# The first sixteen weight pieces on a denser timetable, and v loaded one slot later, in a fused sigmoid attention and bilinear FFN kernel

## The chip, the cores and the metric

The kernel runs on one core of a Trainium2 chip. The metric is device microseconds of one execution. The kernel before was run three times: 1097.2, 1098.67 and 1100.7 us, median 1098.67 us.

## The reference

Float32 throughout. Eight batches of 12 heads, 448 positions, 64 values per head; then an FFN without activation on the 3584 tokens.

```python
scores = scale * np.matmul(q, k.transpose(0, 1, 3, 2)) - np.log(S)
attn = 1.0 / (1.0 + np.exp(-scores))
attn_out = np.matmul(attn, v).astype(np.float32)
x = np.ascontiguousarray(attn_out.transpose(0, 2, 1, 3)).reshape(B * S, H * D)
...
a = x @ w1
b = x @ w2
h = a * b @ w3
return (h @ w_out).astype(np.float32)
```

The weights w1, w2 (768 x 1024), w3 and w_out reach the kernel as the 32-bit words of 64-bit floating point numbers, and the kernel turns them into float32 itself.

## The kernel before, in words

**Attention.** Two heads make a pair, six pairs a batch, 48 pairs in all. A pair's 448 keys are cut into chunks of 128, 128, 128 and 64, taken in the order first, short, second, third. One chunk of one pair is a *slot*; slot number = 4 x pair + place of the chunk. In a slot PE does the score matmuls of its chunk into one of two PSUM tiles `sp` (`scores`, L196 or L199), ACT takes their sigmoid (`attention`, L180), and one slot later PE multiplies it with v (`attend`, L248 or L255, called attend matmuls here). After a pair's last chunk `combine` writes its part of x as a high half `xh` (ACT, L66) and a low half `xl` (DVE, L67).

The first nine pairs (`PLAIN = 9`, slots 0 to 35) do this with plain float32 operands. From pair 9 on (slot 36) every operand is split into a high and a low part: `split_pair` makes qs, kh, kl (DVE L158, L159, L66, POOL L67), `split_v` makes vs, and the sigmoid is taken twice so that DVE can form `al` (L217); the short chunk goes another way (`short_scores` L225, `short_attention` with L187 and L239).

**The up projection.** From slot 26 on, 12 matmuls of `up` (L320) fill each slot: they multiply the x of the batch before with w1 and w2, column block by column block, three slots each. ACT copies one product (`a_sb`, L328), DVE multiplies (`g`, L331), and g goes to DRAM.

**The weights.** w1 and w2 come in 16 pieces: piece 2f is column block f of w1, piece 2f+1 that of w2. `decode_weights` is a generator with two steps a piece. In its first step it issues the load of words to come, lets ACT take the magnitude of this piece and of the next if their words are on the way (`f<-raw`, L79), and issues six DVE instructions (the decode: L86, L91, L94, L98, L99, L102). In its second step it splits the result, with the high half written by ACT (`w<-f`, L66) and the low half by DVE (`w<-f`, L67). The magnitudes lie in two buffers `f`, so the magnitude of a piece waits until the split of the piece two before is over. Pieces 0 to `EARLY - 1` are loaded two pieces ahead into three buffers (768 KB each); the others, and the 16 half-size pieces of w3T that follow, share one buffer, and the load of each stands in the program behind the decode of the piece before.

**What sets the order.** SP (which issues every load and store), PE, ACT and POOL take their instructions in the order in which the program is written, ACT and POOL only until slot 32; the order of DVE, and from slot 32 on that of ACT and POOL, is made by a scheduler when the kernel is built. The list `starts` (L346) gives the slots in which the 16 pieces take their first step, `steps` (L349) adds the second steps (two slots later in the first batch, one later in the second), and `take(weights, steps.count(slot))` (L418) runs them, in each slot behind the sigmoid of that slot. `EARLY` (L351) is worked out from `starts`. `prepare` (L380 on) issues the loads of the pairs to come: q and k two pairs ahead, v one pair ahead into one of two buffers. At slot 32 the three buffers of the early words are given up, and the split operands of pair 9 take their place.

After the attention come the last batch's up projection, w3 times w_out, and the product of g with it.

Of the kernel before, what the change touches and what calls it, by code (L numbers as in the profile page):

```python
# [25 lines left out]
def sigmoid_attention_bilinear_ffn(  # L26
# [29 lines left out]
    PLAIN = 9  # L56
# [66 lines left out]
    def load_pair(b, hp):  # L123
        heads = slice(2 * hp, 2 * hp + 2)
        if b * NPAIR + hp < PLAIN:

            qk = pa.tile([P, 2, S], F32, name="qp", tag="qk", bufs=3)
            for i, src in enumerate((qT, kT)):
                nc.sync.dma_start(out=qk[:, i], in_=src[b, heads].rearrange("h d s -> (h d) s"))
            return qk[:, 0], qk[:, 1]  # L130
        qq = pa.tile([P, 2, S], F32, name="qq", tag="qk", bufs=3)
        kk = pa.tile([P, 2, S], F32, name="kk", tag="qk", bufs=3)
        for dst, src in ((qq, qT), (kk, kT)):
            for r in range(2):
                nc.sync.dma_start(
                    out=dst[r * D:(r + 1) * D], in_=src[b, heads].rearrange("h d s -> d h s")
                )
        return qq, kk

    def load_v(b, hp):  # L140
        vv = pa.tile([P, NC, 2 * D], F32, name="vv")
        cols = slice(hp * 2 * D, (hp + 1) * 2 * D)
        full = (NC - 1) * P
        nc.sync.dma_start(
            out=vv[:, :NC - 1], in_=v[b, :full, cols].rearrange("(c p) e -> p c e", p=P)
        )
        for r in range(1 if b * NPAIR + hp < PLAIN else 2):
            nc.sync.dma_start(out=vv[r * D:(r + 1) * D, NC - 1], in_=v[b, full:, cols])
        return vv

    def split_pair(plain, qq, kk):

        if plain:
            return qq, kk, None, None
        qs = pf[0].tile([P, 2, S], F32R, name="qs")
        kh = pf[0].tile([P, 2, S], F32R, name="kh")
        kl = pf[0].tile([P, 2, S], F32R, name="kl")
        nc.vector.tensor_copy(out=qs, in_=qq)  # L158
        nc.vector.tensor_tensor(out=qs[D:], in0=qq[D:], in1=qs[D:], op=ALU.subtract)  # L159
        split(kh, kl, kk, nc.vector.tensor_copy, nc.gpsimd)  # L160

        ks = pf[0].tile([P, 2, P], F32R, name="ks")
        for j in range(2):
            for i, k in ((j, kh), (1 - j, kl)):
                nc.gpsimd.tensor_copy(out=ks[:, j, i * D:(i + 1) * D], in_=k[:, j, S - D:])
        return qs, kh, kl, ks

    def split_v(plain, vv):
        if plain:
            return vv  # L170

        vs = pf[0].tile([P, NC, 2, 2, D], F32R, name="vs")
        for j in range(2):
            split(vs[:, :, j, j, :], vs[:, :, j, 1 - j, :], vv[:, :, j * D:(j + 1) * D],
                  nc.vector.tensor_copy, nc.gpsimd)
        return vs
# [166 lines left out]
    pairs = [(b, hp) for b in range(B) for hp in range(NPAIR)]  # L343

    first = NPAIR * NC
    starts = [1 + i * first // 7 for i in range(7)] + [first + 1 + 3 * i // 2 for i in range(8)] + [first + 14]  # L346
    assert len(starts) == 2 * NF
    later = [(2 * NPAIR + 2 * i) * NC + 1 for i in range(2 * NF)]
    steps = starts + [s + 2 - s // first for s in starts] + later  # L349
# [29 lines left out]
    def prepare(p, i):  # L379

        n = p + 1
        change = n in (PLAIN, PLAIN + 1)
        if i == (2 if change else 1) and n < len(pairs):
            splits[n] = split_pair(n < PLAIN, *qks.pop(n))
        if i == 0 and change:
            qks[n] = load_pair(*pairs[n])
        if i == (0 if n < PLAIN else 1) and n < len(pairs):
            vvs[n] = load_v(*pairs[n])
        if i == NC - 1 and n < len(pairs):
            vs[n] = split_v(n < PLAIN, vvs.pop(n))  # L390
        n = p + 2
        if i == (0 if n < PLAIN else 2) and n not in (PLAIN, PLAIN + 1) and n < len(pairs):
            qks[n] = load_pair(*pairs[n])
# [6 lines left out]
    for p, (b, hp) in enumerate(pairs):  # L400
        if p == PLAIN - 1:
            order.close()
            order.enter_context(tc.manual_schedule(engines={ET.PE, ET.SP}))
        plain = p < PLAIN
        if p == PLAIN - 1:
            phase_p.close()
            pf.append(phase_a.enter_context(tc.tile_pool(name="pf", bufs=2, side="right")))
        qs, kh, kl, ks = splits.pop(p)
        for i, c in enumerate(chunks):
            prepare(p, i)  # L410
            if not plain and i == 1:
                short = short_scores(ks, qs)
            else:
                sp = scores(qs, kh, kl, c)
                if not plain and i == 2:
                    waiting.append((slot + 1, p, NC - 1, short_attention(short)))
                waiting.append((slot + 1, p, c, attention(plain, sp)))
            take(weights, steps.count(slot))  # L418
            if b > 0 and (hp, i) == (0, 2):
                take(filler, 10 ** 6)  # L420
                filler = up(b - 1, xs[b - 1], itertools.repeat("up"))
            take(filler, ups)
            attend_due(slot)
            slot += 1
# [124 lines left out]
```

## Time and profile before

| | us |
|---|---|
| median of three runs (lowest, highest) | 1098.67 (1097.2, 1100.7) |
| the profiled execution, its own time | 1100.9 |
| its span in the profile | 1099.0 |
| PE busy | 1072.5 |
| DVE busy | 717.4 |
| ACT busy | 564.0 |
| POOL busy | 196.8 |
| granted clock of PE, mean | 0.992 of full |

The span is the profiled execution from its first to its last instruction; 1.9 us lie around it. PE is TensorE's matmuls, PEld its weight loads, DVE VectorE, ACT ScalarE, POOL GpSimd, and SPq the queue through which SyncE issues DMAs. A row of the timeline has the start in us from the span's beginning, the duration, the engine, the line of the code, the operation, what it writes and reads, and in brackets how long the engine had been idle before it and what ended that. A row of the waits has who waited for whom, then the sum in us, the count and the longest. A row of a group has the number of instructions behind the x, the busy time, the mean in ns, and the idle time before. "DMA to landing" is the time from a load's issue to the arrival of its last byte, as lowest, median and highest of the loads asked for. The slots can be found on PE by their score matmuls: slot 9 starts at 24.56, slot 10 at 30.64, slot 26 at 61.95, slot 36 at 106.98, slot 38 at 122.79, slot 40 at 134.15, slot 44 at 158.33 and slot 48 at 173.89 us.

### The profile page before, as it was taken

Reading aid. Unit: us, or ns where it says so; the run is one execution under the profiler, and the core shown is the slowest. Engines: PE = TensorE matmul, PEld = TensorE weight load, DVE = VectorE, ACT = ScalarE, POOL = GpSimd, SP = SyncE. Lnnn points to the kernel's source line nnn. Section 1 sums busy time; section 2 is a strip of 40 time slices with the busy share of each in tenths; the row PEclk is TensorE's granted clock in tenths of the full one; section 3 lists DMA queues with packets and bytes.
Section 4 is the critical chain, followed back from the end, with each engine's and each line's share of the span. In section 5 each row is a group of like instructions: output and inputs, shape, how many; then the busy total and the mean of one; then the engine's idle time right before and its main releaser. Section 6 shows DMA issues by size and latency. Waiting matters only on the chain.

```text
span 1099.0 us, 14114 instructions
## 1 busy us (share of the span) xinstructions
PE 1072.5 (98%) x5076; PEld 913.8 (83%) x5076; DVE 717.4 (65%) x1073; ACT 564.0 (51%) x789; POOL 196.8 (18%) x277
## 2 busy tenths in 40 slices
PE   7999689999999999999999999999999999999998
PEld 1255579999999999899999999999999988888887
DVE  5878787878888887888888877758872122122221
ACT  5753557776677777667776677753342011011100
POOL 0002142333223332332323233300000000000000
PEclk9999899999999999999999999999999999999999
DMA  7562633544444444452543524206462031333211
GB/s 240 165 195 89 151 116 95 132 116 123 114 121 132 114 125 123 108 153 73 151 121 99 161 83 109 73 20 209 140 222 79 10 125 59 123 125 125 86 49 48
DMA packets 100693, 129.15 MB, mean 118 GB/s; under 512 B 8016, under 2 KB 82960, under 8 KB 100624
## 3 DMA queue, kind: packets, MB, share of 16 engines
q1 hardware_dynamic: 100624, 128.25, 39.8%
q8 instruction: 40, 0.66, 0.3%
q14 instruction: 29, 0.24, 0.1%
HBM read 98.34 MB, written 29.88 MB: 117 GB/s over the span
## 4 chain that ended last, share of the span: by engine, by line
PE 85%; DVE 6%; DMA 4%; ACT 2%; issue 2%; SPq 1%; POOL 0%; DVEq 0%; ACTq 0%
PE up L320 38%; PE up L510 21%; PE av L255 10%; PE sp L199 8%; PE up L494 6%; DMA raw<-w 3%; PE sp L225 1%; DVE f L94 1%; ACT f L79 1%; DVE raw L99 1%; DVE f L102 1%; PE av L248 1%; DVE w L67 1%; PE sp L196 1%; DVE raw L86 0%
## 5 line engine op out<-in xcount | busy, mean ns | idle before, releaser
L320 PE MATMUL up<-xh,w 128*128 128x448 f32 x1536 | 469.9, 369 | 1.8 <-DVE g L331 1.8
L320 PEld LDWEIGHTS up<-xh,w 128*128 128x128 f32 x1536 | 290.2, 189 | 34.8 <-issue 5.3
L320 PE MATMUL up<-xl,w 128*128 128x448 f32 x768 | 282.7, 368 | 0.0
L510 PE MATMUL up<-w 128*128 128x512 f32 x1008 | 228.7, 389 | 0.0
L510 PEld LDWEIGHTS up<-w 128*128 128x128 f32 x1008 | 189.2, 188 | 39.3
L180 ACT ACTIVATE ah<-sp,bias 128x896 fp32r<-128x896 f32 x117 | 117.5, 1004 | 114.5 <-PE sp L199 113.7
L67 POOL TENSOR_TENSOR kl<-kk,kh 128x896 fp32r<-128x896 f32 x39 | 88.5, 2268 | 417.9 <-DVE kh L66 401.9
L217 DVE TENSOR_TENSOR al<-sp,ah 128x896 fp32r<-128x896 f32 x117 | 127.3, 1088 | 48.1 <-ACT sp L180 46.7
L320 PEld LDWEIGHTS up<-xl,w 128*128 128x128 f32 x768 | 145.1, 189 | 13.0
L520 DVE COPY o_sb<-up 128x512 f32<-128x512 f32 x42 | 29.0, 690 | 161.1 <-PE up L510 161.1
L66 ACT CAST w<-graw 128x1024 fp32r<-128x1024 f32 x28 | 29.3, 1055 | 174.6 <-PE up L510 170.5
L180 ACT ACTIVATE sp<-sp,bias 128x896 f32<-128x896 f32 x117 | 113.6, 971 | 0.1
L255 PE MATMUL av<-ah,vs 128*128 128x448 f32 x312 | 102.7, 369 | 3.1 <-DVE ah L239 1.3
L199 PE MATMUL sp<-qs,kh 128*128 128x448 f32 x234 | 86.7, 370 | 4.1 <-DVE kh L66 2.4
L67 POOL TENSOR_TENSOR vs<-vv,vs 128x256 fp32r<-128x256 f32 x78 | 70.9, 919 | 99.5 <-DVE vs L66 82.4
L199 PE MATMUL sp<-qs,kl 128*128 128x448 f32 x234 | 86.8, 371 | 1.9 <-POOL kl L67 1.9
L255 PE MATMUL av<-al,vs 128*128 128x448 f32 x234 | 86.0, 368 | 2.1 <-DVE al L217 2.1
L239 DVE TENSOR_TENSOR ah<-st,ah 64x448 fp32r<-64x448 f32 x78 | 57.6, 739 | 21.0 <-ACT st L180 19.2
L255 PEld LDWEIGHTS av<-ah,vs 128*128 128x128 f32 x312 | 58.7, 188 | 10.3 <-issue 3.5
L79 ACT ACTIVATE f<-raw 128x768 f32<-128x768 f32 (+2 forms) x48 | 34.0, 708 | 61.7 <-DMA raw<-w_out 20.7
L186 ACT COPY t<-av 64x448 f32<-64x448 f32 x78 | 41.2, 528 | 33.6 <-PE av L255 32.5
L180 ACT ACTIVATE ah<-st,bias 64x448 fp32r<-64x448 f32 x78 | 52.2, 669 | 4.0 <-DVE st L187 2.1
(54 smaller groups left out, 1249.0 us busy)
## 6 DMA issues: line engine op xcount, KB each, us to landing
qq<-qT SPq DMA_DIRECT2D x78, 224.0 KB, 3.9
kk<-kT SPq DMA_DIRECT2D x78, 224.0 KB, 4.4
g_dram<-g SPq DMA_DIRECT2D x64, 224.0 KB, 2.0
graw<-g_dram SPq DMA_DIRECT2D x14, 1024.0 KB, 5.4
raw<-w SPq DMA_DIRECT2D x16, 768.0 KB, 6.5
out<-o_sb SPq DMA_DIRECT2D x42, 256.0 KB, 2.0
vv<-vL SPq DMA_DIRECT2D x48, 192.0 KB, 2.7
raw<-w3T SPq DMA_DIRECT2D x16, 512.0 KB, 4.3
```

Source lines behind the costliest of these rows:

```text
L66: hi_engine(out=dst_hi, in_=src)
L67: lo_engine.tensor_tensor(out=dst_lo, in0=src, in1=dst_hi, op=ALU.subtract)
L79: nc.scalar.activation(f, raw[..., 1].bitcast(F32), AF.Abs, scale=HW_SCALE)
L180: nc.scalar.activation(dst, src, AF.Sigmoid, bias=bias[:n], scale=scale)
L186: nc.scalar.copy(out=dst[rows], in_=src[j][others])
L199: nc.tensor.matmul(sp[:, j], k[:, j, at:at + n], qs[:, j], start=m == 0, stop=m == 1)
L217: nc.vector.tensor_tensor(out=al, in0=sp, in1=ah, op=ALU.subtract)
L239: nc.vector.tensor_tensor(out=a[others, j], in0=t[rows], in1=a[rows, j], op=ALU.subtract)
L255: nc.tensor.matmul(accs[j][:, :S], v[:, c, j].rearrange("p u d -> p (u d)"), a[:, j], start=first and m == 0, stop=last and m == len(ops) - 1,
L320: nc.tensor.matmul(acc[:, :S], w[:, fc, kc], x, start=(kc == 0 and m == 0), stop=(kc == NK - 1 and m == 2),)
L494: nc.tensor.matmul(acc[:, :NM], a[:, jc], w[:, jc, ms], start=(jc == 0 and m == 0), stop=(jc == NF - 1 and m == 2),)
L510: nc.tensor.matmul(acc[:, :TB], w[:, fc, ms], g[:, at, fc % NH], start=(fc == 0 and m == 0), stop=(fc == NF - 1 and m == 2),)
```

## The change

```diff
     first = NPAIR * NC
-    starts = [1 + i * first // 7 for i in range(7)] + [first + 1 + 3 * i // 2 for i in range(8)] + [first + 14]
+    starts = [1 + 3 * i for i in range(8)] + [first + 1 + 4 * i // 3 for i in range(8)]
     assert len(starts) == 2 * NF
...
         if i == 0 and change:
             qks[n] = load_pair(*pairs[n])
-        if i == (0 if n < PLAIN else 1) and n < len(pairs):
+        if i == 1 and n < len(pairs):
             vvs[n] = load_v(*pairs[n])
```

The first steps of the 16 pieces move from slots 1, 4, 7, 11, 14, 18, 21, 25, 26, 28, 29, 31, 32, 34, 35, 38 to slots 1, 4, 7, 10, 13, 16, 19, 22, 25, 26, 27, 29, 30, 31, 33, 34. The second steps move from 3, 6, 9, 13, 16, 20, 23, 26, 27, 29, 30, 32, 33, 35, 36, 39 to 3, 6, 9, 12, 15, 18, 21, 24, 26, 27, 28, 30, 31, 32, 34, 35. `EARLY` becomes 14 instead of 12. The w3T pieces keep their slots. The loads of v for the first nine pairs are issued in the second slot of the pair before instead of its first; those of the later pairs were there already.

On SP, in slots 4 to 7: `qp` is q and k of pair 3, `vv` is v of pair 2, `raw` on w2 is piece 3's words, and the row ahead of them is piece 2's. Before:

```order
L74 DMA raw_122<-w1 128x6x256
L144 DMA vv_153<-vL 128x3x128
L148 DMA vv_153<-vL 64x128
L129 DMA qp_156<-qT 128x448
L129 DMA qp_156<-kT 128x448
L74 DMA raw_164<-w2 128x6x256
```

After:

```order
L74 DMA raw_122<-w1 128x6x256
L129 DMA qp_153<-qT 128x448
L129 DMA qp_153<-kT 128x448
L74 DMA raw_161<-w2 128x6x256
L144 DMA vv_177<-vL 128x3x128
L148 DMA vv_177<-vL 64x128
```

The loads of v, which need the buffer of pair 0's v, moved from ahead of q, k and piece 3's words to behind them.

On DVE, around slot 36, whose `al` is the L217 row. `f_730` and `f_769` are pieces 13 and 14 before; a `w` row is the low half of a split. Before:

```order
L102 TENSOR_TENSOR f_730<-f_730,raw_663 128x768
L331 TENSOR_TENSOR g_752<-up_703,a_sb_701 128x448
L67 TENSOR_TENSOR w_90<-f_730,w_89 128x768
L86 TENSOR_SCALAR raw_738<-raw_738 128x768
L91 TENSOR_SCALAR f_769<-f_769 128x768
L94 SCALAR_TENSOR_TENSOR f_769<-f_769,raw_738 128x768
L98 TENSOR_SCALAR raw_738<-f_769 128x768
L217 TENSOR_TENSOR al_808<-sp_800,ah_805 128x896
L99 SCALAR_TENSOR_TENSOR raw_738<-raw_738 128x768
L67 TENSOR_TENSOR xl_830<-av_710,xh_829 128x448
L102 TENSOR_TENSOR f_769<-f_769,raw_738 128x768
```

After, where `f_707` is piece 14, `f_754` is piece 15 and `raw_762` the first piece of w3T:

```order
L102 TENSOR_TENSOR f_707<-f_707,raw_640 128x768
L66 CAST vs_781<-vv_698 128x4x64
L67 TENSOR_TENSOR w_88<-f_707,w_87 128x768
L331 TENSOR_TENSOR g_776<-up_725,a_sb_723 128x448
L86 TENSOR_SCALAR raw_715<-raw_715 128x768
L91 TENSOR_SCALAR f_754<-f_754 128x768
L94 SCALAR_TENSOR_TENSOR f_754<-f_754,raw_715 128x768
L98 TENSOR_SCALAR raw_715<-f_754 128x768
L99 SCALAR_TENSOR_TENSOR raw_715<-raw_715 128x768
L102 TENSOR_TENSOR f_754<-f_754,raw_715 128x768
L67 TENSOR_TENSOR w_90<-f_754,w_89 128x768
L217 TENSOR_TENSOR al_822<-sp_814,ah_819 128x896
```

The end of piece 14 and all of piece 15, which stood behind slot 36's al, now stand ahead of it; behind it the first w3T piece follows at once.

On DVE in the first batch, the rows at the turn from one piece to the next, where `f_248` is piece 4, `f_291` piece 5 and `raw_289` the words of piece 6; after:

```order
L102 TENSOR_TENSOR f_291<-f_291,raw_246 128x768
L67 TENSOR_TENSOR w_88<-f_248,w_87 128x768
L86 TENSOR_SCALAR raw_289<-raw_289 128x768
L67 TENSOR_TENSOR xl_339<-av_299,xh_338 128x448
L91 TENSOR_SCALAR f_328<-f_328 128x768
```

and before, at the same turn:

```order
L102 TENSOR_TENSOR f_299<-f_299,raw_253 128x768
L67 TENSOR_TENSOR w_88<-f_255,w_87 128x768
L67 TENSOR_TENSOR xl_332<-av_289,xh_331 128x448
L86 TENSOR_SCALAR raw_297<-raw_297 128x768
L91 TENSOR_SCALAR f_350<-f_350 128x768
```

The xl of a pair moved at this turn from ahead of the next piece's decode to inside it; the split of piece 4 stays behind the decode of piece 5 in both.

## The prediction

> **What bounds the kernel now.** I read the page's busy shares first, then the table of windows, cut at the score matmuls of slots 26, 36, 44 and 48.
>
> ```profile
> span 1099.0 us, 14114 instructions
> PE 1072.5 (98%) x5076; PEld 913.8 (83%) x5076; DVE 717.4 (65%) x1073; ACT 564.0 (51%) x789; POOL 196.8 (18%) x277
> ```
>
> ```profile
> 0.00:61.95 61.95, 52.15 (x204) 12.97 (x204) 43.96 (x62) 40.84 (x49) 0.20 (x4) 0.97 0.65 202
> 61.95:106.98 45.03, 45.03 (x202) 26.50 (x201) 34.49 (x50) 20.82 (x27) 5.02 (x6) 1.00 0.50 142
> 106.98:158.33 51.35, 39.13 (x155) 31.71 (x154) 41.55 (x57) 26.28 (x36) 13.62 (x16) 0.87 0.45 119
> 158.33:173.89 15.56, 15.56 (x78) 14.26 (x76) 12.36 (x20) 10.74 (x15) 6.03 (x8) 1.00 0.41 115
> 173.89:700.00 526.11, 525.40 (x2568) 481.58 (x2567) 428.88 (x642) 375.54 (x534) 167.26 (x238) 1.00 0.44 118
> ```
>
> The columns are the stretch, its length, then busy time of PE, PEld, DVE, ACT and POOL, granted clock, DMA share, GB/s. From slot 44 (158.33) on, PE has no gap, so whatever moves slot 44 moves the end by as much. Slots 26 to 36 are full too (45.03 of 45.03, 4.50 a slot). The loss is elsewhere: 9.8 us of PE idle before slot 26, and slots 36 to 44 took 51.35 where eight later slots take 2 x 15.56 = 31.1: 20.2 us. The change touches only these stages. Next the timeline of the first loss:
>
> ```profile
> 17.31 0.38 SPq L144 DMA_DIRECT2D vv<-vL  x1
> 19.43 1.08 SPq L74 DMA_DIRECT2D raw<-w  x2
> 23.61 0.95 DVE L67 TENSOR_TENSOR w<-f,w 128x768 fp32r<-128x768 f32 x1
> 24.56 0.97 PE L196 MATMUL sp<-qp 64*64 64x448 f32 x4
> 27.40 0.89 ACT L79 ACTIVATE f<-raw 128x768 f32<-128x768 f32 x1 [4.40 <-DMA raw<-w]
> 29.23 1.48 PE L248 MATMUL av<-ap,vv 128*64 128x448 f32 x4 [3.70 <-ACT ap L180]
> 30.64 1.86 PE L196 MATMUL sp<-qp 64*128 64x448 f32 x4
> ```
>
> SP stood before v of pair 2 until 17.31, so piece 3's words were issued at 19.43. ACT stood before their magnitude (L79) until 27.40, the sigmoid behind it came late, and PE lost 3.70 us and then its clock (four matmuls 1.86 instead of 0.97). Now the second loss:
>
> ```profile
> 115.82 0.89 ACT L79 ACTIVATE f<-raw 128x768 f32<-128x768 f32 x1 [3.53 <-DMA raw<-w]
> 119.28 1.08 DVE L217 TENSOR_TENSOR al<-sp,ah 128x896 fp32r<-128x896 f32 x1
> 122.65 0.37 SPq L74 DMA_DIRECT2D raw<-w  x1
> 122.66 0.83 ACT L66 CAST w<-f 128x768 fp32r<-128x768 f32 x1 [2.74 <-DVE f L102]
> 134.15 0.44 PE L199 MATMUL sp<-qs,kh 128*128 128x448 f32 x1 [2.36 <-DVE kh L66]
> 140.90 0.95 DVE L67 TENSOR_TENSOR w<-f,w 128x768 fp32r<-128x768 f32 x1
> ```
>
> The last pieces share one buffer, so each load waits for the decode before it (piece 15's at 122.65), and the last split of weights (140.90) comes 21 us after slot 36's al (119.28), between the conversions that PE waits for.
>
> **The change part by part.** *v one slot later.* q and k of pair 3 and piece 3's words now stand ahead of v of pair 2 on SP. They wait for no attend matmul, so they go by 17.3 instead of 19.43; piece 3 landed 8 us after issue, so by 25.3 at the latest. Magnitude 3 then waits for its buffer f: split 1 ends at 24.56. I take 24.6; 2.8 us gained on 27.40. The cost I take at nothing: v's first use is still four slots (7.8 us at the 1.96 below) behind its issue, and the words that it is now queued behind wait only for a decode that ended a whole loop (below) earlier; without that cover it would cost PE the landing, some 5 us.
>
> *Pieces every third slot.* They meet a loop, whose rows are these:
>
> ```profile
> 49.07 0.90 ACT L79 ACTIVATE f<-raw 128x768 f32<-128x768 f32 x1
> 50.00 0.56 DVE L86 TENSOR_SCALAR raw<-raw 128x768 uint32<-128x768 uint32 x1 [0.57 <-ACT f L79]
> 54.52 0.97 DVE L67 TENSOR_TENSOR w<-f,w 128x768 fp32r<-128x768 f32 x1
> 55.52 0.92 ACT L79 ACTIVATE f<-raw 128x768 f32<-128x768 f32 x1 [0.60 <-DVE w L67]
> ```
>
> The next magnitude needs the f buffer that the split behind this decode frees: 55.52 - 49.07 = 6.45 a piece, about 7.0 where the order puts an xl (0.62, row below) inside. Slots 10 to 26 took (61.95 - 30.64) / 16 = 1.96, so three are 5.9 and the loop is now the longer. From magnitude 3 at 24.6, three turns with xl and two without bring magnitude 8 to 24.6 + 21.0 + 12.9 = 58.5. It stands at slot 22; its 0.9 and the sigmoid's 1.0 hold the attend matmuls in slot 24, then 0.97 and one slot: slot 26 at 63.2, 1.2 later than now. The stall saved is more than given back, but one piece more is done. Slots 26 to 36 keep their 45.0: slot 36 at 108.2.
>
> *The second batch.* From magnitude 9 (58.5 + 6.45 = 64.95, decode from 65.9) DVE has to do, until slot 36's al, by these groups (DVE until 160 us, mean ns):
>
> ```profile
> L331 DVE TENSOR_TENSOR g<-up,a_sb 128x448 f32<-128x448 f32 x6 | 3.7, 617 | 0.6 <-PE up L320 0.6
> L67 DVE TENSOR_TENSOR xl<-av,xh 128x448 fp32r<-128x448 f32 x9 | 5.6, 621 | 0.0
> L159 DVE TENSOR_TENSOR qs<-qq,qs 64x896 fp32r<-64x896 f32 x4 | 6.2, 1542 | 0.1
> L158 DVE CAST qs<-qq 128x896 fp32r<-128x896 f32 x4 | 2.5, 622 | 0.0
> L66 DVE CAST kh<-kk 128x896 fp32r<-128x896 f32 x4 | 2.5, 621 | 0.0
> L66 DVE CAST vs<-vv 128x256 fp32r<-128x256 f32 x6 | 2.3, 393 | 0.0
> ```
>
> Seven decodes of 54.52 - 50.00 = 4.52 (31.6), eight splits of 0.96 (7.7), three g, two xl and pair 9's q, k, v (6.7): 46.0. DVE is then nearly full and its waits count:
>
> ```profile
> 62.38 0.97 SPq L74 DMA_DIRECT2D raw<-w  x2
> DMA to landing us min/median/max: 8.9/8.9/8.9
> ...
> DMA to landing us min/median/max: 5.4/5.4/5.4
> ...
> DMA to landing us min/median/max: 4.3/4.3/4.3
> ```
>
> ```profile
> 99.52 1.90 DVE L67 TENSOR_TENSOR w<-f,w 128x768 fp32r<-128x768 f32 x1 [0.90 <-ACT w L66]
> 134.08 2.33 POOL L67 TENSOR_TENSOR kl<-kk,kh 128x896 fp32r<-128x896 f32 x1 [25.36 <-DVE kh L66]
> ```
>
> ```profile
> L180 ACT ACTIVATE ah<-sp,bias 128x896 fp32r<-128x896 f32 x117 | 117.5, 1004 | 114.5 <-PE sp L199 113.7
> ```
>
> The landings are those of the first load at 62.38, of the one at 122.65 and of a w3T load. Piece 10 goes out near 62.5 with piece 11 close behind, lands 8.9 later at 71.4, and its decode waits 1.7. Magnitude 13 follows split 11 with nothing between: 0.95. Pieces 13 and 14 are now loaded ahead; piece 15 waits for decode 14: 5.4 and 0.95, less 2.8 of other work, 3.6. After decode 15 the cast (0.83), ah and its sp (1.0 each) must pass before al: 2.0 beyond split 15. A DVE pass beside POOL took 1.90 instead of 0.95; bounds 0 and 2, I take 0.5. So al starts at 65.9 + 46.0 + 1.7 + 0.95 + 3.6 + 2.0 + 0.5 = 120.6 (now 119.28), with all weights behind it.
>
> *Slots 38 to 44.* The w3T load waits for decode 15 (117.7), lands 4.3 after its issue, its magnitude ends near 123.0. Then come eleven DVE steps (6.8) to kh of pair 10 at 129.8, and kl (2.3) at 132.1; beside it L239 and al for slot 39, to about 133. Slot 40 starts at 133.5, against 134.15 now. From there nothing of the weights is left in DVE's way except a half-size piece: 15.6 to slot 44 instead of 158.33 - 134.15 = 24.2. The sum: 0.65 + 8.6 = 9.3 us. Against the profiled execution's own 1100.9 us (2.2 above the median) that is 1091.6; against the median 1098.67, **1089.4 us**. Later steps keep their slots, and PE has no gap there.
>
> The Trainium skill, "DMA: Bandwidth & Descriptors", section "Queues, rings and completion order", says that each DMA engine consumes its descriptors in ring order. By it piece 11 behind could not slow piece 10, and the sum would be 11.0, giving 1087.7; no row shows it, as other loads ran ahead of 62.38 too, so I keep 8.9.
>
> **The rivals.** *A, slower: PE's clock in the first batch.* Rows on what an idle PE does:
>
> ```profile
> 111.11 0.47 PE L320 MATMUL up<-xh,w 128*128 128x448 f32 x1 [1.82 <-DVE g L331]
> 112.47 0.58 PE L320 MATMUL up<-xl,w 128*128 128x448 f32 x1
> 151.90 0.44 PE L199 MATMUL sp<-qs,kh 128*128 128x448 f32 x1 [1.73 <-DVE st L187]
> ```
>
> In each of the five loops PE idles 0.6 to 1.1. If that takes its clock, as 1.82 did (0.58 a matmul behind it), six groups of four cost 0.85 more each, 5.1 a loop, about 4 beyond its slack: 20 us over five loops, less 9.3: 1109. It decides from more than two slow loops on. Against it: after 1.73 idle the 151.90 row still shows 0.44. The Trainium skill, "TensorE: Matmul & The Clock Gate", section "Part 1: The HAM clock gate (the "warmup" mystery)", puts the limit at an idle window of about 3.4 us; the 1.82 row falls short of that and slowed all the same, so I leave A 6 in 100.
>
> *B: the idle returns in slots 40 to 44.* q, k and v of pair 10 now stand on SP behind the w3T load, issued near 118. At a landing like the 8.9 they come at 127, at the moment when qs needs them; pair 11's follow. If half of the 8.6 is lost again, the gain is 4.7 less the rest: 1094.0. For it: PE's 2.36 wait for kh above. Against: SP is free of that load 5 us sooner than now. 17 in 100.
>
> *C: DVE's waits are smaller.* No wait for piece 10, none beside POOL, and slot 40 a microsecond sooner: 1.7 + 0.5 + 1.0 more, 1086.2. 15 in 100.
>
> That the change doesn't do what it says is excluded by the order, in which the decodes do move.
>
> **How the numbers follow.** The forecast's own range, from the ends of its unknown costs, is 1087.0 to 1092.5, at 58 in 100; 4 are left for no effect. The range takes in C and B with a microsecond or two: 1085.0 to 1096.0; A and no effect stay out. A measurement of this kernel can tell about 0.3% (3.3 us) from no change. Faster: forecast, C and half of B, 0.80; within it: the rest of B, no effect and the forecast's slow tail, 0.13; slower: A and a little, 0.07.
>
> **What would show it.** Right: no ACT wait for raw near 24 and PE's 3.70 gone; magnitudes 6.4 to 7.1 apart until slot 22; slot 26 near 63; last split of weights ahead of slot 36's al, near 120; slot 40 near 133.5 and slot 44 near 149. Wrong: matmuls of 1.8 for four in the first batch (A), PE waits for kh or qs after slot 40 (B), or slot 36 not full-speed behind slot 26.

## The result, and the profile after

The changed kernel took 1089.68 us (median of six runs, 1088.86 to 1090.5), the kernel before 1099.49 us in the same comparison (six runs, 1097.2 to 1101.67): a ratio of 0.991, with a 95% interval of 0.9896 to 0.9925, or 9.8 us less. In a later comparison the same two kernels stood at 1091.44 and 1098.65 us: 0.9938 (0.9919 to 0.9956), 7.2 us less. Both intervals lie beyond the 0.3% that can be told from no change, and the forecast of 1089.4 us lies between the two results.

The profiled execution of the changed kernel took 1088.86 us, with this span and these busy shares on its page:

```profile
span 1087.0 us, 14111 instructions
PE 1067.2 (98%) x5076; PEld 911.4 (84%) x5076; DVE 720.1 (66%) x1073; ACT 563.6 (52%) x789; POOL 194.6 (18%) x277
```

PE's busy time fell by 5.3 us though it issues the same 5076 matmuls: what went is time in which matmuls ran at a lower clock. The windows of the profile show a granted clock of 0.50 before from 29.57 to 32.98, 111.49 to 114.90, 121.73 to 125.14 and 135.38 to 142.21, 17.1 us in all, and after only from 118.28 to 125.10, 6.8 us; half of the difference is 5.1. So of the 12.0 us between the two profiled spans 5.3 are the clock's, and 6.7 are idle time of PE. The table of windows, cut as in the prediction at the score matmuls of slots 26, 36 and 44, with the columns explained there:

```profile
0.00:62.45 62.45, 50.95 (x205) 12.76 (x205) 47.32 (x66) 42.20 (x51) 0.20 (x4) 1.00 0.72 220
62.45:107.47 45.02, 45.02 (x203) 26.50 (x201) 41.56 (x56) 21.58 (x28) 6.38 (x7) 1.00 0.49 144
107.47:146.64 39.17, 34.98 (x155) 29.71 (x154) 32.81 (x45) 23.69 (x33) 10.22 (x14) 0.91 0.47 122
```

Slot 26 comes 0.5 us later than before, slots 26 to 36 last the same 45.02, and slots 36 to 44 last 39.17 instead of 51.35. All of the gain up to slot 44 is in that third row. DVE did 41.56 us of work in the stage before it (34.49 before): the decodes have moved from where PE waited for them to where they had room.

The first loss, in the timeline (rows that answer to those of the prediction):

```profile
15.02 0.38 SPq L74 DMA_DIRECT2D raw<-w  x1
...
16.87 0.38 SPq L144 DMA_DIRECT2D vv<-vL  x1
...
24.34 0.91 ACT L79 ACTIVATE f<-raw 128x768 f32<-128x768 f32 x1 [1.79 <-DVE w L67]
...
26.20 0.97 PE L248 MATMUL av<-ap,vv 128*64 128x448 f32 x4 [1.11 <-ACT ap L180]
27.10 1.02 PE L196 MATMUL sp<-qp 64*128 64x448 f32 x4
```

Piece 3's words go out at 15.02, ahead of v. Its magnitude waits for the split (`w L67`), no longer for its words, and the matmuls behind PE's short wait take 1.02 for four, not 1.86. Then PE's waits up to 160 us, as who waited for whom, sum, count and longest:

```profile
PE av L248 <- ACT ap L180: 6.7, 6, 1.3
...
PE av L255 <- DVE al L217: 1.5, 1, 1.5
PE av L255 <- DVE xl L67: 1.4, 1, 1.4
PE av L255 <- ACT ah L180: 1.3, 1, 1.3
```

The one wait of 3.70 has become six of at most 1.3, one behind each magnitude from piece 3's to piece 8's; the waits for `kh`, `kl` and `st` in slots 40 to 44 are gone.

### The profile page after: what moved, and what is told of

The parts are those of the page before. It is cut to its first block, busy times and chain, and to the rows that moved or that the text cites. A ratio compares the mean times of both kernels' runs of the same rounds, so it can differ in the third digit from the quotient of the medians.

```text
span 1087.0 us, 14111 instructions
## 1 busy us (share of the span) xinstructions
PE 1067.2 (98%) x5076; PEld 911.4 (84%) x5076; DVE 720.1 (66%) x1073; ACT 563.6 (52%) x789; POOL 194.6 (18%) x277
## 4 chain that ended last, share of the span: by engine, by line
PE 86%; DVE 9%; DMA 2%; issue 1%; ACT 1%; SPq 1%; DVEq 0%; ACTq 0%
PE up L320 39%; PE up L510 21%; PE av L255 10%; PE sp L199 8%; PE up L494 6%; DVE f L94 1%; PE sp L225 1%; DVE raw L99 1%; DVE w L67 1%; ACT f L79 1%; DVE raw L86 1%; DVE raw L98 1%; DVE f L91 1%; DVE f L102 1%; DVE al L217 0%
## 5 line engine op out<-in xcount | busy, mean ns | idle before, releaser
L67 POOL TENSOR_TENSOR kl<-kk,kh 128x896 fp32r<-128x896 f32 x39 | 87.3, 2238 | 407.6 <-DVE kh L66 407.6
L320 PEld LDWEIGHTS up<-xl,w 128*128 128x128 f32 x768 | 144.6, 188 | 12.9
L217 DVE TENSOR_TENSOR al<-sp,ah 128x896 fp32r<-128x896 f32 x117 | 127.4, 1089 | 42.0 <-ACT sp L180 40.8
L67 POOL TENSOR_TENSOR vs<-vv,vs 128x256 fp32r<-128x256 f32 x78 | 71.3, 925 | 100.1 <-DVE vs L66 79.4
L239 DVE TENSOR_TENSOR ah<-st,ah 64x448 fp32r<-64x448 f32 x78 | 60.2, 772 | 21.2 <-ACT st L180 19.4
```

What stands on the lines that cost most here:

```text
L67: lo_engine.tensor_tensor(out=dst_lo, in0=src, in1=dst_hi, op=ALU.subtract)
L217: nc.vector.tensor_tensor(out=al, in0=sp, in1=ah, op=ALU.subtract)
L239: nc.vector.tensor_tensor(out=a[others, j], in0=t[rows], in1=a[rows, j], op=ALU.subtract)
L320: nc.tensor.matmul(acc[:, :S], w[:, fc, kc], x, start=(kc == 0 and m == 0), stop=(kc == NK - 1 and m == 2),)
```

## The experiments

All times are in us. The kernels ran in three comparisons, each with the kernel before on the same chip (medians 1098.23, 1098.54 and 1098.65). The second table cuts each profiled execution at PE's score matmuls; it starts at slot 9 because the time until there differs between executions of one and the same kernel (last section).

| kernel | median | ratio to before | 95% interval |
|---|---|---|---|
| v later, old timetable | 1091.88 | 0.9940 | 0.9917 to 0.9962 |
| new timetable, v as before | 1095.76 | 0.9977 | 0.9958 to 0.9995 |
| first batch's timetable (and v) | 1094.65 | 0.9969 | 0.9953 to 0.9985 |
| second batch's timetable (and v) | 1095.92 | 0.9978 | 0.9962 to 0.9994 |
| changed, third f buffer | 1084.00 | 0.9866 | 0.9845 to 0.9886 |
| v later, old timetable, third f buffer | 1087.71 | 0.9905 | 0.9888 to 0.9921 |
| changed, no load of piece 15 | 1091.48 | 0.9931 | 0.9916 to 0.9946 |
| changed, w3T's load later | 1093.67 | 0.9958 | 0.9943 to 0.9974 |
| both of these | 1091.78 | 0.9939 | 0.9923 to 0.9955 |
| changed, 15 early pieces | 1086.80 | 0.9886 | 0.9866 to 0.9907 |
| third f buffer and 15 early pieces | 1080.37 | 0.9835 | 0.9818 to 0.9852 |
| changed, again | 1091.44 | 0.9938 | 0.9919 to 0.9956 |

| profiled execution | slot 9 at | 9-26 | 26-36 | 36-40 | 40-44 | 9-44 |
|---|---|---|---|---|---|---|
| before | 24.56 | 37.39 | 45.03 | 27.17 | 24.18 | 133.77 |
| changed | 24.12 | 38.33 | 45.02 | 23.27 | 15.90 | 122.52 |
| changed, again | 28.02 | 37.86 | 45.03 | 23.38 | 16.02 | 122.29 |
| v later, old timetable | 24.87 | 33.25 | 45.02 | 24.27 | 24.32 | 126.86 |
| new timetable, v as before | 25.11 | 42.19 | 45.61 | 24.52 | 15.54 | 127.86 |
| first batch's timetable | 25.96 | 37.65 | 45.03 | 23.85 | 21.26 | 127.79 |
| second batch's timetable | 24.28 | 33.26 | 45.02 | 30.73 | 20.34 | 129.35 |
| third f buffer | 28.19 | 31.25 | 45.02 | 20.26 | 16.18 | 112.71 |
| v later, third f buffer | 26.43 | 31.26 | 45.03 | 22.98 | 22.39 | 121.66 |
| no load of piece 15 | 25.19 | 38.23 | 45.03 | 23.94 | 15.53 | 122.73 |
| w3T's load later | 27.66 | 37.85 | 45.02 | 22.93 | 15.57 | 121.37 |
| both of these | 24.61 | 38.20 | 45.03 | 20.35 | 15.56 | 119.14 |
| 15 early pieces | 28.05 | 37.80 | 47.26 | 16.99 | 15.56 | 117.61 |
| third f buffer, 15 early | 27.79 | 31.26 | 46.23 | 18.28 | 15.53 | 111.30 |

### Which half of the change makes the gain

First, the kernel before with v one slot later and nothing else:

```diff
-        if i == (0 if n < PLAIN else 1) and n < len(pairs):
+        if i == 1 and n < len(pairs):
```

> The old timetable, v one slot later. My theory: the stall near slot 9 shrinks from 3.7 us to about 1, slot 26 comes 2 to 4 us earlier, but the chain of single-buffer loads of pieces 13 to 15 and decodes 14 and 15 behind slot 36's al stay, so that most of the loss after slot 36 stays: 1095 to 1097. Rival 1 (v's slot is the gain): 1090.

Measured: 1091.88, 6.4 below before. The theory had 1095 to 1097 and missed; the rival, by which v is the larger part of the gain, was nearer. PE's waits in this kernel, up to 170 us:

```profile
PE sp L199 <- DVE kh L66: 2.6, 1, 2.6
PE av L255 <- DVE al L217: 2.5, 1, 2.5
PE sp L199 <- POOL kl L67: 2.3, 1, 2.3
...
PE sp L199 <- DVE st L187: 1.7, 1, 1.7
PE av L248 <- ACT ap L180: 1.7, 2, 0.9
```

The waits for `ap` are down to two of at most 0.9, and slots 9 to 26 take 33.25 instead of 37.39: 4.1 us saved there. I had thought that the old second batch would use such a lead up; it did not: slots 26 to 36 take the same 45.02, and slots 36 to 44 even less than before, 48.59. The waits for `kh`, `kl` and `st` in slots 40 to 44 are all still there (24.32).

Second, the reverse: the new timetable with v in its old place.

```diff
-        if i == 1 and n < len(pairs):
+        if i == (0 if n < PLAIN else 1) and n < len(pairs):
```

> The new timetable alone, v loaded in its old slot. My theory (the loop from magnitude to magnitude and DVE's chain carry any delay of piece 3 through to slot 40): the words of piece 3 go out behind v of pair 2 again, near 19, magnitude 3 comes near 27 instead of 24.3, and the 2.7 us stay: about 1092.4, PE waiting over 3 us near slot 9. Rival 1 (the gain comes from v's slot): back to 1097 or more. Rival 2 (the later load cost nothing and brought nothing): 1089.7.

Measured: 1095.76, 2.5 below before, between theory and rival. The timeline at the two places where SP's order matters:

```profile
19.98 1.07 SPq L74 DMA_DIRECT2D raw<-w  x2
...
27.52 0.89 ACT L79 ACTIVATE f<-raw 128x768 f32<-128x768 f32 x1 [3.99 <-DMA raw<-w]
29.36 1.18 PE L248 MATMUL av<-ap,vv 128*64 128x448 f32 x4 [3.29 <-ACT ap L180]
30.47 1.87 PE L196 MATMUL sp<-qp 64*128 64x448 f32 x4
...
55.92 0.89 ACT L79 ACTIVATE f<-raw 128x768 f32<-128x768 f32 x1 [2.95 <-DMA raw<-w]
57.76 0.97 PE L248 MATMUL av<-ap,vv 128*64 128x448 f32 x4 [2.25 <-ACT ap L180]
```

Piece 3's words go out at 19.98 again, the stall on them is back, with the slow matmuls behind it (1.87 for four), and a second of the same kind stands at 57.76. Slots 9 to 26 take 42.19. Slots 40 to 44 take 15.54: that gain belongs to the timetable.

So the two halves do different work. Put onto the kernel with v moved, the timetable costs 38.33 - 33.25 = 5.1 us in slots 9 to 26, and saves 48.59 - 39.17 = 9.4 in slots 36 to 44, a net 4.3. Of this 1.2 is lost again between slots 44 and 52, which take 32.33 against 31.15 with v alone. The medians show still less: 0.9940 for v alone against 0.9910 and 0.9938 for the whole change. In the one comparison that has each half alone, v gains 6.4 and the timetable 2.5, with intervals that hardly overlap, so v is the larger part there; how much the timetable adds to it lies between almost nothing and 3 us by the medians.

### Which half of the timetable

The changed kernel with the old spacing in the second batch, and with the old spacing in the first:

```diff
-    starts = [1 + 3 * i for i in range(8)] + [first + 1 + 4 * i // 3 for i in range(8)]
+    starts = [1 + 3 * i for i in range(8)] + [first + 1 + 3 * i // 2 for i in range(8)]
```

```diff
-    starts = [1 + 3 * i for i in range(8)] + [first + 1 + 4 * i // 3 for i in range(8)]
+    starts = [1 + i * first // 7 for i in range(7)] + [first + 1 + 4 * i // 3 for i in range(9)]
```

> Pieces 0 to 7 every third slot, the rest at the old spacing (slots 25, 26, 28, 29, 31, 32, 34, 35), v one slot later. Thirteen pieces are loaded ahead. My theory: DVE is full from slot 26 on, so the slots matter little, but pieces 14 and 15 both wait for the shared buffer, one wait of 3 us more: 1092 to 1093. Rival 2 (what counts is how dense the second batch is): 1096 or more.

> Pieces 0 to 6 in their old slots, nine pieces in the second batch at 4/3 slots (25 to 35), v one slot later. My theory: slot 26 comes about 3 us earlier than in the changed kernel (fewer turns of the loop), but DVE has one piece (6 us) more to do behind it and one more single-buffer wait: al of slot 36 and slot 40 about 3 us later, 1092 to 1093. Rival 2 (the dense second batch is the gain): 1090 or less.

Measured: 1094.65 and 1095.92, both above their forecasts, and both slower than with v alone in the same comparison, by 2.8 us, at which the intervals still overlap a little, and by 4.0. The waits of the second:

```profile
PE sp L199 <- DVE kh L66: 5.6, 1, 5.6
...
PE av L255 <- DVE xl L67: 3.5, 1, 3.5
```

With seven pieces in the first batch, nine are left for the second; the last takes its first step in slot 35, and slots 36 to 40 take 30.73. With eight and the old second spacing, slots 9 to 26 pay the 37.65 and slots 40 to 44 still take 21.26. Neither half by itself brings slots 40 to 44 near 15.6; both together do.

### Is the loop over the two f buffers what is paid in the first batch

The changed kernel, where the early pieces but the last take the magnitude's buffer from the pool of three in which their words lie (the last three pieces keep the two old buffers, so that there are five in all):

```diff
-    def magnitude(raw):
-        f = pd.tile([P, *raw.shape[1:-1]], F32, name="f")
+    def magnitude(raw, early=False):
+        if early:
+            f = pp.tile([P, *raw.shape[1:-1]], F32, name="fe")
+        else:
+            f = pd.tile([P, *raw.shape[1:-1]], F32, name="f")
...
-                    fs[k] = magnitude(raws[k])
+                    fs[k] = magnitude(raws[k], k < EARLY - 1)
```

> The changed kernel with three buffers f instead of two for the early pieces. My theory: the loop (a magnitude waits for the split of the piece two before) is what stretches the first batch to 6.45 to 7.0 us a piece. Without it PE's waits of about 1 us before slots 11 to 24 go, slot 26 comes 2 to 4 us earlier (58.5 to 60.5 instead of 62.45), and since DVE's chain starts earlier by about as much, 1086 to 1088. Rival (DVE's work itself, 5.95 us a piece, or ACT's fills the time): slot 26 within 1 us of 62.45 and 1089 to 1090.

Measured: 1084.00, better than the 1086 to 1088 of the theory. The lines of the code stand three lower here, so that the magnitude is L82. The timeline of ACT, and the window of slots 9 to 26:

```profile
37.78 0.92 ACT L82 ACTIVATE fe<-raw 128x768 f32<-128x768 f32 x1
...
43.10 0.90 ACT L82 ACTIVATE fe<-raw 128x768 f32<-128x768 f32 x1
```

```profile
28.19:59.44 31.25, 31.25 (x138) 7.93 (x136) 30.57 (x44) 26.97 (x34) 0.00 (x0) 1.00 0.72 220
```

No magnitude waits for a split; these two are 5.3 apart where three slots of 31.25 / 17 = 1.84 are 5.5, and PE is busy for all 31.25. So the loop over two buffers was what the new timetable paid, 7 us of it, and DVE has the time for a piece every three slots: it is busy for 30.57 of the 31.25, without PE waiting.

The same buffer with v moved and the old timetable tells whether the new timetable is worth anything once the buffer is there:

> The old timetable with v one slot later and three buffers f. If the loop is the price that the denser timetable pays in the first batch, the old timetable has little to gain from a third buffer: slots 9 to 26 go from 33.3 us to 31.3 at most, slots 36 to 44 keep 48 to 49, 1090 to 1092. Rival (the third buffer helps by itself, whatever the timetable): 1086.

Measured: 1087.71; the rival's 1086 was nearer than the theory's 1090 to 1092. The old timetable met the loop too, since slots 9 to 26 go from 33.25 to 31.26. The new timetable still shortens slots 36 to 44 from 45.37 to 36.44, and its ratio of 0.9866 (0.9845 to 0.9886) stands below 0.9905 (0.9888 to 0.9921), though in another comparison.

### What still stands in slots 36 to 44

Four kernels ask what the 39.17 us there are made of, where 31.1 would be PE's own. By the table of windows above 4.2 us of the rest are PE's idle time (39.17 - 34.98), and the other 3.9 are mostly its slower clock, 6.8 us at half. In the first, piece 15 takes over the buffer of piece 14's words as they are and nothing is loaded for it: the last column block of w2 is not computed. In the second, the first w3T piece is loaded in that piece's own first step, not behind decode 15. The third does both.

```diff
-            f = decode(raws.pop(i), fs.pop(i))
-            if i + 1 >= EARLY and i + 1 < len(jobs):
+            raw = raws.pop(i)
+            f = decode(raw, fs.pop(i))
+            if i + 1 == 2 * NF - 1:
+                raws[i + 1] = raw
+            elif i + 1 >= EARLY and i + 1 < len(jobs):
```

```diff
+            if i == 2 * NF:
+                load_job(i)
...
-            if i + 1 >= EARLY and i + 1 < len(jobs):
+            if i + 1 >= EARLY and i + 1 < len(jobs) and i + 1 != 2 * NF:
```

> The changed kernel, with the words of piece 15 not loaded: it decodes piece 14's buffer a second time, so the last column block of w2 is not the reference's. My theory: DVE's 3.06 us wait before decode 15, behind the load that waits for decode 14, is on the path; slot 36's al comes 3 to 4.5 us earlier and slot 40 by 2 to 3: 1087. Rival (PE's own work or the conversions of pair 10 set slot 40): 1089 to 1090.

> The changed kernel with the first w3T piece loaded in its own slot (49) instead of behind decode 15. My theory: its load stands before pair 10's q and k on SP, its magnitude holds ACT, and its decode (4.3 us of DVE) stands between slot 36's al and pair 10's conversions; without it slot 40 comes 2 to 3 us earlier: 1087 to 1088. Rival (that work is covered): 1089 to 1090.

> The run without piece 15's load (its decode reads piece 14's buffer again, so the last column block of w2 is not the reference's) had the first w3T decode ahead of slot 36's al, which hides what the wait costs. Here that piece also waits for its own slot 49. If the wait before decode 15 is on the path, slots 36 to 44 take 35 to 36 us instead of the 38.5 of the run with w3T late alone, and the time is 2 to 3 us below that run: 1091. Rival (the wait is covered): 38 us and 1093 to 1094.

The first settled nothing (1091.48, above both forecasts; 39.47 in slots 36 to 44): with decode 15 ready sooner, the scheduler put the w3T piece's decode ahead of slot 36's `al`, and PE waited 2.3 us for that. The second was wrong: 1093.67 where 1087 to 1088 was expected. Slots 36 to 44 took 38.50, 0.7 less, and a new wait came much later, in the timeline:

```profile
189.31 2.38 POOL L67 TENSOR_TENSOR kl<-kk,kh 128x896 fp32r<-128x896 f32 x1 [8.61 <-DVE kh L66]
...
189.74 2.90 DVE L159 TENSOR_TENSOR qs<-qq,qs 64x896 fp32r<-64x896 f32 x1
...
194.65 0.44 PE L199 MATMUL sp<-qs,kh 128*128 128x448 f32 x1 [2.61 <-DVE st L187]
```

So the w3T load is not what holds slots 36 to 44, and a later decode of it costs more elsewhere: behind slot 44 this kernel takes 944.4 us, the changed kernel 940.3. Since the third differs from the second by the load of piece 15 alone, those two make the cleaner comparison: 35.91 against 38.50 us in slots 36 to 44, where 35 to 36 was expected, and 1091.78 where 1091 was. The windows of these slots, second kernel first:

```profile
110.53:149.03 38.50, 34.86 (x155) 30.01 (x154) 29.63 (x40) 23.15 (x32) 9.00 (x14) 0.91 0.44 111
```

```profile
107.84:143.75 35.91, 32.35 (x155) 27.85 (x153) 28.41 (x38) 22.20 (x31) 9.03 (x14) 1.00 0.44 111
```

Without the load of piece 15 these slots are 2.6 us shorter. But PE is idle for 3.6 us in both, 38.50 - 34.86 and 35.91 - 32.35: what went is busy time, at a clock of 1.00 instead of 0.91. The wait for piece 15's words cost PE its clock here, and not more idle time.

The fourth kernel removes that wait in the right way, by a timetable in which piece 14 comes two slots earlier, so that piece 15 is loaded two slots ahead of its decode, with 15 early pieces instead of 14:

```diff
-    starts = [1 + 3 * i for i in range(8)] + [first + 1 + 4 * i // 3 for i in range(8)]
+    starts = [1 + 3 * i for i in range(8)] + [first + 1 + i for i in range(7)] + [first + 9]
```

> The changed kernel with pieces 8 to 14 in every slot from 25 to 31 and piece 15 in slot 33: fifteen pieces loaded ahead, none waits for the shared buffer. My theory: the 3.06 us wait before decode 15 goes as in the run without its load, and DVE was full before it anyway: 1087 to 1088. Rival (the denser second batch holds ACT, and so PE's sigmoids, before slot 36): PE waits between slots 26 and 36 and 1090 or more.

Measured: 1086.80, as expected (1087 to 1088). PE's waits up to 150 us:

```profile
PE up L320 <- ACT a_sb L328: 2.2, 1, 2.2
...
PE av L255 <- DVE xl L67: 0.7, 1, 0.7
```

Of the waits in slots 36 to 44 only 0.7 is left (32.55 us there, at full clock), and the denser second batch costs one wait of 2.2 for `a_sb` in slots 26 to 36 (47.26 instead of 45.02).

### Both remedies together

The third f buffer and the 15 early pieces in one kernel:

> Three buffers f for the early pieces, and fifteen pieces before slot 32 (pieces 8 to 14 in every slot from 25 to 31, piece 15 in slot 33). If the loop in the first batch and the wait for piece 15 are two separate losses, as my theory has it, they add: 5.7 and 2.9 us below the changed kernel's 1089.7 give 1081; slots 36 to 44 near 32.5 us. Rival (both only start DVE's chain earlier, so that one is enough): 1084, as with three buffers alone.

Measured: 1080.37 (1079.37 to 1080.72), where the theory by which the two losses add had 1081. Its windows, for slots 9 to 26, 26 to 36 and 36 to 40:

```profile
27.79:59.05 31.26, 31.26 (x139) 7.93 (x137) 30.60 (x43) 27.03 (x34) 0.00 (x0) 1.00 0.75 227
59.05:105.28 46.23, 45.10 (x202) 26.50 (x201) 45.89 (x64) 24.49 (x32) 2.71 (x2) 1.00 0.54 157
105.28:123.56 18.28, 16.44 (x78) 13.66 (x77) 14.73 (x23) 10.42 (x15) 6.79 (x13) 1.00 0.52 131
```

Slots 9 to 44 take 111.30, and the clock is full in all of these rows. This version beats both kernels: 18.3 us below the kernel before, 11.1 below the changed kernel in the same comparison. DVE's 45.89 of 46.23 says that there is no more room in slots 26 to 36.

### The changed kernel once more

> The changed kernel once more, for a second profile on the chip of these runs. Both theories: 1088.5 to 1091. If the stretch up to slot 9 differs by over a microsecond between the two profiles while the rest agrees, the difference of 12.0 us between the two profiled executions is partly a matter of the start.

Measured: 1091.44, just above what was expected. From slot 9 to slot 44 the two executions of it agree within 0.3 us (122.52 and 122.29); slot 9 stands at 24.12 in the one and 28.02 in the other, and the spans, 1087.0 and 1090.6, differ by nearly as much.

## Why the prediction was right, step by step

**v one slot later: right, and worth more than it was given.** Piece 3's words went at 15.02 (by 17.3 was forecast), magnitude 3 at 24.34 (24.6). The 2.8 us taken for it is only the magnitude's own lead; what PE's 3.70 and the slow matmuls behind it cost in slots 9 to 26 is 4.1, as the kernel with v alone shows, and the whole of that kernel's gain is 6.4. The prediction never named the two halves' shares, and its sum hides that: it counted the stall's end and the loop's price as one difference of 1.2 at slot 26. They are -4.1 and +5.1, a net of 1.0.

**The loop: right, and shown by taking it away.** The five turns run from magnitude 3 at 24.34, shown above, to magnitude 8; the other row is magnitude 10's:

```profile
57.90 0.89 ACT L79 ACTIVATE f<-raw 128x768 f32<-128x768 f32 x1 [1.96 <-DVE w L67]
...
68.79 0.93 ACT L79 ACTIVATE f<-raw 128x768 f32<-128x768 f32 x1 [1.94 <-DVE w L67]
```

They took 57.90 - 24.34 = 33.56 (33.9 was forecast), and slot 26 came at 62.45 (63.2). The third buffer removed it: 31.25 in place of 38.33.

**The second batch: a step that failed.** Slot 36's `al` started at 117.07, not 120.6. "Piece 10 ... its decode waits 1.7" did not happen: the last row above, magnitude 10, waits for a split and not for its words. The load issued at 61.77, with piece 11's close behind it, shows this landing:

```profile
L74 SPq DMA_DIRECT2D raw<-w x1: 1152/1152/1152, 61.8 to 61.8; - x1
...
DMA to landing us min/median/max: 5.6/5.6/5.6
```

It landed in 5.6, not in the 8.9 of the row I took. By the Trainium skill, "DMA: Bandwidth & Descriptors", section "Queues, rings and completion order", each DMA engine takes its descriptors in ring order; by that a load behind would not slow the one ahead. The trace agrees: this load had piece 11's 1.69 us behind it, and the one at 81.06, with another 0.43 behind it, landed in 5.2. I had chosen the wrong one of the two figures. Why the load at 62.38 took 8.9 before stays open: the loads ahead of it had landed 2.9 us after its issue, those ahead of this one 2.5. The other terms, in DVE's timeline:

```profile
101.05 2.19 DVE L66 CAST vs<-vv 128x256 fp32r<-128x256 f32 x1
...
109.78 0.56 DVE L86 TENSOR_SCALAR raw<-raw 128x768 uint32<-128x768 uint32 x1 [3.06 <-ACT f L79]
...
115.29 0.96 DVE L67 TENSOR_TENSOR w<-f,w 128x768 fp32r<-128x768 f32 x1 [0.90 <-ACT w L66]
117.07 1.09 DVE L217 TENSOR_TENSOR al<-sp,ah 128x896 fp32r<-128x896 f32 x1 [0.82 <-ACT sp L180]
...
125.29 3.08 DVE L239 TENSOR_TENSOR ah<-st,ah 64x448 fp32r<-64x448 f32 x2
```

The wait for piece 15 was 3.06 (3.6), the tail behind its split 0.82 (2.0), and a pass beside POOL cost 2.19 - 0.39 = 1.8 where I took 0.5. Together with the 0.6 by which magnitude 9 came sooner these are 0.6 + 1.7 + 0.54 + 1.18 - 1.3 = 2.7 of the 3.5. The rest is DVE's work: from decode 9's start at 65.26 to `al` it was busy for 44.6 us, 42.8 without the 1.8, where the sum had 46.0. Against that stand waits that the sum left out, 0.66 and 0.90 before the last two splits among them, for ACT's high halves.

**Slots 38 to 44: near in time, but not by the path that it named.** Slot 40 stands at 130.74 (133.5), 13.67 behind `al` where the prediction had 12.9. The prediction let slot 40 wait for pair 10's `kl` and slot 39's `al`. PE waited for neither. `kl` was done at 127.89, and `al` at 129.49, 0.6 us before PE took it, though another pass beside POOL, the pair at 125.29, had taken 3.08. From 120.31 to 138.00 PE was busy throughout, until 125.10 at half clock (last section): what set slot 40 was PE's own work, at a clock whose fall the prediction had left out here. That the two lengths are so close is luck. Slots 40 to 44 took 15.90 (15.6), so slot 44 came at 146.64 (149.1). Slots 44 to 52 then took 178.97 - 146.64 = 32.33 instead of twice 15.56: 1.2 of the lead was lost there, though the prediction had nothing lost behind slot 44.

**The sum.** At slot 52 the kernel is 1.2 us ahead of the forecast for this execution, and behind slot 52 it took 1.6 less than the kernel before (1087.0 - 178.97 = 908.0 against 909.6). That makes the 2.7 between 1088.86 and the 1091.6 expected of the profiled execution. By medians, 9.3 was forecast and 9.8 and 7.2 measured. The difference of the profiled spans, 12.0, is least fit to judge by, for it holds the start-up of single executions. In slots 9 to 44 the gain is 133.77 - 122.52 = 11.3, more than either median shows. A late start that the kernel before makes good in its stall on piece 3, and the changed kernel does not, would explain that; no run tested it.

That 1089.4 lies between the two medians is in part luck. For the profiled execution the same sum was 2.7 us too high, and on the way it missed by more: `al` came 3.5 us sooner than forecast, and what the prediction had at nothing, the half clock behind `al` and the 1.2 us behind slot 44, took back over half of that. And the range of 1085 to 1096 is wide: v alone, and either half of the timetable beside it, fall inside it too.

**The rivals.** A fell: six idles of 0.87 to 1.29 in the first batch, and behind them four matmuls in 0.97 and 1.02. It was not far off, though: in the kernel with the first batch's timetable alone, whose first batch is the same, the granted clock was 0.50 from 48.66 to 52.08. B, the idle returning in slots 40 to 44, is not to be seen: PE waits for neither `kh` nor `qs` there; DVE waits once for v, 0.71. C was right on piece 10 and wrong on POOL, where it had no cost and 1.8 appeared.

## What to carry to other kernels

A denser timetable for side work pays only as far as the buffers let the work run: here two buffers in rotation made a loop of 6.45 to 7.0 us that no timetable of 5.5 us could beat, and a third was worth more than the retiming itself. Before costing such a change, look in each stage for what the next piece really waits for, a buffer, a load or the slot, and try the halves alone, because each half of this timetable, put beside the moved v, was slower than no change of it. PE's idle time can cost as much again in clock: 2.8 us of it between 114.86 and 118.28 were followed by 6.8 us at half clock, a loss of some 3.4. What stands first in the queue that issues loads can matter as much: one slot for v was worth 6.4 us.

## What the runs showed of the hardware that was not expected

**Some DVE passes beside POOL wait until POOL is done.** POOL's rows at the two places:

```profile
100.40 2.69 POOL L67 TENSOR_TENSOR kl<-kk,kh 128x896 fp32r<-128x896 f32 x1 [99.96 <-DVE kh L66]
...
125.34 2.55 POOL L67 TENSOR_TENSOR kl<-kk,kh 128x896 fp32r<-128x896 f32 x1 [18.55 <-DVE kh L66]
```

The cast of 2.19 ends at 103.24, POOL's pass at 103.09; the pair of 3.08 ends at 128.37, 0.48 behind POOL's 127.89. So they end with POOL's pass or shortly behind it, as if they had stood still beside it. The Trainium skill, "SBUF — State Buffer", section "SBUF: two separate sides", says that the port pair that VectorE and GpSimd share is locked for a whole instruction, and the other engine blocks; it says so of certain VectorE passes, among them those with two inputs in SBUF against a GpSimd pass that reads SBUF. The trace agrees: `g` and `al`, which read one input from PSUM, keep their length beside POOL. The `al` at 128.40, with POOL busy until 129.00, took 1.09, and all 117 of them took 1.08 to 1.09; the 64 of `g` took 0.61 to 0.63. The price of one meeting is, by my estimate, up to a whole POOL pass of some 2.6 us; the largest shown here is 1.8.

**PE's clock fell behind two short idles.** In slots 36 to 38 PE shows these rows:

```profile
116.31 0.44 PE L255 MATMUL av<-ah,vs 128*128 128x448 f32 x1 [1.33 <-ACT ah L180]
...
118.22 0.72 PE L255 MATMUL av<-al,vs 128*128 128x448 f32 x1 [1.47 <-DVE al L217]
...
120.31 0.71 PE L255 MATMUL av<-ah,vs 128*128 128x448 f32 x1 [1.38 <-DVE xl L67]
...
121.20 0.57 PE L199 MATMUL sp<-qs,kh 128*128 128x448 f32 x1
```

The first matmul behind the first idle takes 0.44, later ones 0.57. The windows around the fall:

```profile
114.86:118.28 3.42, 0.62 (x3) 0.25 (x2) 2.05 (x2) 2.74 (x5) 0.00 (x0) 1.00 0.80 247
118.28:121.69 3.41, 2.03 (x5) 1.48 (x6) 2.79 (x6) 2.45 (x5) 0.00 (x0) 0.50 1.10 246
```

The clock, the third number from the end, fell at 118.28, behind the second idle and before the third, and stayed at half for 6.82 us. All stretches at half clock that are named in the section on the result last 3.41 us or twice that. In all 14 traces the changes of the clock lie on a grid of 3.41 us. Cut by this grid, the first 220 us show 20 falls of the clock: 16 stand behind a stretch in which PE was busy for at most 0.27 of it (here 0.18, or 0.62 of 3.42 us), and 4 behind one of 0.47 to 0.62. No emptier stretch than 0.47 left the clock full; between 0.47 and 0.62 some did and some did not. So the idle time in such a stretch decides, and not the length of one idle. In the first batch of the changed kernel the emptiest stretch, at 43.18, was busy for 2.12 of 3.41, 0.62, and the clock stayed. The Trainium skill's limit of an idle window of about 3.4 us ("TensorE: Matmul & The Clock Gate", section "Part 1: The HAM clock gate (the "warmup" mystery)") fits the length of these stretches, but all except one of the 20 had PE busy for a part of them.

**The clock at the start rises at different times.** Four score matmuls take about 1.86 at the lower clock and 1.02 at the full one. In the first profiled execution of the changed kernel the first row at 1.02 is this:

```profile
13.04 1.02 PE L196 MATMUL sp<-qp 64*128 64x448 f32 x4
```

In the second, four are still partly slow here:

```profile
18.37 1.46 PE L196 MATMUL sp<-qp 64*128 64x448 f32 x4
```

By the trace's record of the clock the rise comes at 12.46 in the one and at 19.28 in the other, 6.82 or two stretches later, and slot 9 at 24.12 and 28.02. All 14 traces go this way: where the rise comes between 12.46 and 13.60, slot 9 starts at 24.12 to 25.19 (seven traces), and where it comes between 18.78 and 20.32, at 27.66 to 28.19 (five). In the other two it comes at 7.7, is lost for one stretch from 14.5 on, and slot 9 starts at 25.96 and 26.43. The same page and section of the Trainium skill say that the window is free-running and that the point varies by about 500 ns; here it varied by 6.8 us between two executions of one kernel. Whoever compares two profiled executions of this kernel has to cut them behind slot 9.
